# An unread F32 matmul behind each pair's channel transforms, with 71 to 64 columns

## The chip, the cores and the metric

The kernel runs on one core of a Trainium2 chip. The metric is the device time of one execution in microseconds (us). Profiled executions come with a trace of every instruction on the engines TensorE (PE; its weight loads are listed apart as PEld), VectorE (DVE), ScalarE (ACT), GpSimd (POOL) and SyncE (SP).

## The reference

```python
x = A_x                                    # (1, 2048, 512), float32
xn = _layernorm(x)
s = irfft2(rfft2(xn) * (A_w_r + 1j * A_w_i))      # over tokens and channels
h = _layernorm(xn)                         # inside the token MLP
u = gelu(einsum("bsd,sf->bdf", h, w1) + b1)       # w1: 2048 x 1792
y = einsum("bdf,fs->bds", u, w2) + b2             # w2: 1792 x 2048
out = x + s * silu(y.transpose(0, 2, 1))
```

Two things are computed from the same normalised tokens: a spectral filter (a two-dimensional FFT, a product with weights, and the inverse), and an MLP over the tokens, whose result gates the first.

## The kernel before

The 2048 tokens are 16 blocks of 128, the 512 channels stay whole. A first stage (to about 203 us) normalises the tokens, multiplies them with w1 into the hidden units, and does the token transforms and the filter of the spectral part between these products. From there on stands the last stage, with the second product of the MLP, the way back from channel frequencies to channels, the gates and the output.

The last stage (line 1038) is a loop over 8 pairs: pair p is the token blocks p and p + 8. For one pair the product with w2 is done in seven smaller products (names 1, 2, 5, 6, 3, 7, 4 of `ORDER`, line 800), sums of blocks of w2 against sums of blocks of the hidden units. `products` (line 905) issues one of them as 21 matmuls of 128 x 128 by 128 x 256: seven blocks of hidden units, each three times, since both sides are split into a high and a low part in F32R. In the trace these are `fa`, `fb`, `fc` or `fd` (hidden units) with `w2f` (the split weight). ScalarE and VectorE make the next `w2f` while TensorE works. The first two products of pair 0 are issued ahead of the loop.

Once in each pair, behind the product with the number `slot` (the 7th in pair 0, the 6th in pairs 1 to 6, the 4th in pair 7; `SLOTS`, line 38), TensorE does a few products in plain F32, in the order that `PARTS` (line 44) gives for the pair:

- E, `even_channels` (line 966): sixteen matmuls of 64 x 64 by 64 columns, `cd,yt` in the trace (`ci` is the tile `cd`, filled anew with other constants). Those of pair 0 are issued one product earlier (line 1075).
- S, `spectral` (line 1006): four matmuls of 64 x 64 by 512 columns for the pair before, `y,cft`. Pair 0 has none; pair 7's own come later (line 1096), ahead of its last product.
- O, `odd_channels` (line 977): four matmuls of 128 x 128 by 128 columns, `cd,yt`. They are the last of the group in every pair.

Then `unfolded` (line 984) reads the banks 6 and 7 of PSUM on ScalarE and VectorE, and from pair 1 on `finish` (line 1022) multiplies the pair before with its gates and adds it to the output by DMA. The seven products write the left halves (256 of 512 columns) of bank 4, of bank 5, and of bank 2 or 3 in turn (`banks`, line 902). The right half of bank 4 is not used in this stage.

In this stage instructions stand on each engine in the order in which they are written (`Kept`, line 131). Every instruction that goes through that helper has line 139 in the trace.

Of the kernel before, what the change touches and what calls it, by code (L numbers as in the profile page):

```python
# [141 lines left out]
def spectral_mixer_kernel(tc, x, w1, b1, w2, b2, wk, we, wx, c_f, c_ft, c_d, c_i, c_g, c_h, out):  # L142
    nc = tc.nc
    V, A, G, T, SY = nc.vector, nc.scalar, nc.gpsimd, nc.tensor, nc.sync
# [17 lines left out]
    with tc.tile_pool(name="ps", bufs=1, space=PSUM) as psp, ExitStack() as left, ExitStack() as right:  # L162
        ps = psp.tile([P, 8, 512], F32, name="ps")
# [297 lines left out]
        T = Kept(T, keep)  # L461
# [46 lines left out]
        for j in range(NJ):  # L508
# [25 lines left out]
            start, more_stats = j < 3, j + 3 < NJ  # L534
# [264 lines left out]
        NP, HD = NJ // 2, D // 2  # L799
# [38 lines left out]
        def sums_of_blocks():  # L838
            added_up("a12", "s1")
            added_up("a11", "a12")  # L840
# [36 lines left out]
        ci = cd  # L877
# [24 lines left out]
        def banks(p):  # L902
            return ps[:, 3 - p % 2, :HD], ps[:, 4, :HD], ps[:, 5, :HD]

        def products(p, n):

            wf = ready.pop(0)
            bx, by, bz = banks(p)
            o = {1: bx, 6: bx, 7: bx, 4: bx, 2: by, 5: bz, 3: bz}[n]

            for a, (wi, ui) in enumerate(((0, 0), (0, 1), (1, 0))):
                for m, i in enumerate(FORMS):
                    T.matmul(o, wf[:, wi, i], form_parts(n, i)[ui], start=m + a == 0 and n in (1, 2, 5),
                             stop=m == NH - 1 and a == 2, skip_group_check=n in (6, 3, 7, 4))

        def copied(name, src, where):
            t = where.tile([P, HD], F32, name=name, tag=name.split("_")[0], bufs=1)
            step(A.activation(t, src, AF.Copy))
            return t
# [21 lines left out]
        def new_sums(p):  # L941
            return (fp.tile([P, 2, 2, 2, P], F32, name=f"es{p}", tag="es"),
                    fp.tile([P, 2, 2, 2, P], F32, name=f"y{p}", tag="y"))

        def new_gates(p):
            return [fp.tile([P, D], F32, name=f"g{j}", tag="g", bufs=4) for j in (p, p + NP)]
# [6 lines left out]
        def gathered(p):  # L953


            yt = fp.tile([P, 2, 4, 2, 64], F32, name=f"yt{p}", tag="yt")
            yts[p] = yt
            for i, j in enumerate((p, p + NP)):
                for h in range(2):
                    to = yt[:, i, :, h ^ i].rearrange("p b (s c) -> p b s c", c=2)  # L960
                    yield V.tensor_copy(to, ey[:, :, h::2, j]) if i else A.activation(to, ey[:, :, h::2, j], AF.Copy)
# [4 lines left out]
        def even_channels(p):  # L966


            for i in range(2):
                for s in range(2):  # L970
                    at = slice(128 * i + 64 * s, 128 * i + 64 * s + 64)
                    for e in range(2):
                        for r, rows in enumerate((slice(0, 64), slice(64, P))):
                            T.matmul(ps[64 * e:64 * e + 64, 6 + r, at], yts[p][rows, i, 2 * s, e], ci[rows, 2 * s, :64],
                                     start=True, stop=True)
# [8 lines left out]
        def unfolded(p):  # L984

            es, y = new_sums(p) if p else first_sums
            e0, e1 = (es[:, :, k].rearrange("p i b c -> p i (b c)") for k in range(2))
            first, odd = ps[:, 6, :256].rearrange("p (i s c) -> p i s c", s=2, c=64), ps[:, 6:8, 256:]
            other = y.rearrange("p i h q c -> p (i h q c)")[:, :257]
            A.activation(other, ps[:, 7, :257], AF.Copy)  # L990
            other = other[:, :256].rearrange("p (i s c) -> p i s c", s=2, c=64)

            V.tensor_add(es[:, :, 1, :, :64], first, other)
            V.tensor_sub(es[:, :, 1, 0, :63:-1], first[:, :, 0], other[:, :, 0])
            V.tensor_sub(es[:, :, 1, 1, :63:-1], other[:, :, 1], first[:, :, 1])
            V.tensor_add(e0, e1, odd)
            V.tensor_sub(e1, e1, odd)
            yield
            u, v = es[:, :, :, 0], es[:, :, :, 1]
            V.tensor_add(y[:, :, :, 0], u, v)  # L1000
            yield
            V.tensor_sub(y[:, :, ::-1, 1], u, v)
            ys[p] = y.rearrange("p i h q c -> p i (h q c)")
            yield

        def spectral(p):

            y = ys.pop(p)
            for e, cols in enumerate((slice(0, 64), slice(64, P))):
                for r, rows in enumerate((slice(0, 64), slice(64, P))):  # L1010
                    i = e ^ r
                    T.matmul(ps[cols, i], cft[rows, cols], y[rows, i], start=True, stop=True)

        def gate(g, j, cols, src, scale):
            A.activation(g[:, cols], src, AF.Silu, bias=b2t[:, j:j + 1], scale=scale)

        def summed(name, a, b):
            t = fp.tile([P, HD], F32, name=name, tag="c", bufs=2)
            V.tensor_add(t, a, b)
            return t  # L1020
# [17 lines left out]
        for p in range(NP):  # L1038
            j0, j1 = p, p + NP
            more = p + 1 < NP  # L1040
            if p:
                gates[p] = new_gates(p)
            g0, g1 = gates[p]
            bx, by, bz = banks(p)
            slot, plan = SLOTS[min(p, 2) + (not more)]
            gathering = gathered(p)
            for k, n in enumerate(ORDER):
                started = not p and k < 2
                if not started:
                    products(p, n)  # L1050
                if n == 1 and p:
                    p1 = copied(f"p1_{p}", bx, w2p)
                elif n == 5:
                    p5 = copied(f"p5_{p}", bz, fp)
                elif n == 6:
                    v2 = copied(f"v2_{p}", bx, fp)
                elif n == 7:
                    c22 = summed(f"c22_{p}", bx, p5)
                if n == 3 and more:
                    c12 = summed(f"c12_{p}", bz, v2)  # L1060
                if not started:
                    ready.extend(w for w in [next(wforms, None)] if w is not None)
                if n == 2:
                    c11 = summed(f"c11_{p}", by, p1)
                elif n == 6:
                    gate(g0, j0, left_, c11, 1.0)
                elif n == 3 and more:
                    gate(g0, j0, right_, c12, 1.0)
                elif n == 7:
                    gate(g1, j1, right_, c22, -1.0)  # L1070
                elif n == 4:
                    for cols in (left_,) if more else quarter_rows:
                        gate(g1, j1, cols, bx[:, cols], -1.0)
                if not p and k == slot - 1:
                    even_channels(p)
                if k == slot:
                    for part in PARTS[p]:
                        {"S": spectral, "E": even_channels, "O": odd_channels}[part](p - (part == "S"))
                    yts.pop(p)
                    pieces = unfolded(p)  # L1080
                    if p:
                        for g, j in zip(gates.pop(p - 1), (j0 - 1, j1 - 1)):
                            finish(g, j, whole)
                for what in plan.get(k, ""):
                    next(gathering if what == "g" else pieces)
                if n == 3 and not more:
                    gate(g0, j0, right_, summed(f"c12_{p}", bz, v2), 1.0)
                if more and n == 7:
                    sums_of_blocks()
                if not more and k == 2:  # L1090
                    xr = [where.tile([P, NH * P], F32, name=f"xr{i}", tag="s1", bufs=1)[:, :D] for i, where in enumerate((w2p, fp))]
                    for to, j in zip(xr, (j0, j1)):
                        for rows, tokens in halved:
                            SY.dma_start(to[rows], x[tokens, j])
                if not more and k == 5:
                    spectral(p)
                    last_rows = fp.tile([P, 2, D], F32, name="rows", tag="yt")
                    finish(g0, j0, whole)
                    finish(g1, j1, right_)
# [38 lines left out]
```

## Time and profile before

| | |
|---|---|
| three runs, us | 365.52, 365.53, 365.69 |
| median | 365.53 |
| profiled execution, us | 365.77 |
| its span, first to last instruction | 364.0 |
| TensorE matmuls, busy | 358.1 us (98%), 3476 records |
| TensorE weight loads, busy | 310.8 us (85%) |
| VectorE, ScalarE, GpSimd, busy | 307.8, 211.2, 87.2 us |
| mean granted TensorE clock | 1.000 |

The profiled execution's own time is 1.77 us above its span. Busy times of matmuls overlap, and so do those of weight loads with matmuls: how fast TensorE moves is read from the starts of its instructions. One F32 matmul of the code can be several records of the trace; the count in a row of the order of instructions is that of the code, the count in a row of the trace that of the records.

### The profile page before, as it was taken

What the parts mean: (1) busy time and instruction counts of PE and PEld (TensorE: products, weight loads), DVE (VectorE), ACT (ScalarE), POOL (GpSimd) and SP (SyncE); (2) the same over time, 40 slices, a digit from 0 to 9 for tenths busy, and PEclk for the clock granted to TensorE, in tenths of its full rate; (3) what the DMA queues carried; (4) which work ended last, traced back from release to release, by engine and by line L of the source; (5) the groups of instructions that cost most, each with busy time, mean ns of one, the idle gap of its engine ahead of it and who ended that gap; (6) DMA issues with size and microseconds to landing.
All of it is one profiled execution on the core that took longest, in us unless ns stands there. A gap on an engine that the chain in (4) does not pass through costs nothing.

```text
span 364.0 us, 8851 instructions
## 1 busy us (share of the span) xinstructions
PE 358.1 (98%) x3476; PEld 310.8 (85%) x3476; DVE 307.8 (85%) x590; ACT 211.2 (58%) x385; POOL 87.2 (24%) x134
## 2 busy tenths in 40 slices
PE   8999999999999999999999999999999999999994
PEld 7788888888877778777888999989898989898993
DVE  5899999967699997999995988687887878797974
ACT  4877778867634426755237884655464546565431
POOL 4233333323222012220120001040503132130330
PEclk9999999999999999999999999999999999999999
DMA  7977999306695687996577288698888989898624
GB/s 207 246 190 187 231 288 333 133 0 155 172 275 181 189 241 193 252 239 201 174 236 156 101 236 172 180 185 200 189 184 212 178 224 164 240 162 209 114 27 90
DMA packets 33293, 68.66 MB, mean 189 GB/s; under 512 B 4612, under 2 KB 19380, under 8 KB 33124
## 3 DMA queue, kind: packets, MB, share of 16 engines
q1 hardware_dynamic: 24276, 42.44, 42.2%
q0 software_dynamic: 8496, 25.01, 32.0%
q10 hardware_dynamic: 480, 0.66, 0.6%
q8 instruction: 27, 0.44, 0.6%
q14 instruction: 14, 0.11, 0.1%
HBM read 59.70 MB, written 8.13 MB: 186 GB/s over the span
## 4 chain that ended last, share of the span: by engine, by line
PE 96%; DVE 1%; DMA 1%; issue 0%; ACT 0%; DVEq 0%
PE ps L139 96%; DMA x<-in_x_dram 1%; DVE stm L244 0%; DVE rows L139 0%; DVE h L469 0%; DVE w1l L469 0%; DVE h L272 0%; ACT g L139 0%; DVE v2m L221 0%; DVE mvm L220 0%; DVE tm L229 0%; ACT sdm L223 0%; DVEq L1134 0%; DVE r0m L228 0%; DVE nbm L237 0%
## 5 line engine op out<-in xcount | busy, mean ns | idle before, releaser
L139 PE MATMUL ps<-h,w1h 128*128 128x512 f32 x400 | 116.3, 397 | 0.1
L139 PEld LDWEIGHTS ps<-h,w1h 128*128 128x128 f32 x400 | 72.9, 188 | 19.9 <-issue 4.9
L139 PE MATMUL ps<-h,w1l 128*128 128x512 f32 x200 | 67.6, 390 | 0.0
L139 DVE TENSOR_TENSOR w2f<-a,w2f 128x896 fp32r<-128x896 f32 x36 | 39.2, 1090 | 16.4 <-ACT w2f L139 16.4
L139 ACT ACTIVATE w2f<-a 128x896 fp32r<-128x896 f32 x36 | 37.2, 1033 | 20.0 <-PE ps L139 7.6
L139 PEld LDWEIGHTS ps<-h,w1l 128*128 128x128 f32 x200 | 37.5, 188 | 8.1
L139 PE MATMUL ps<-fb,w2f 128*128 128x256 f32 x336 | 42.1, 280 | 0.0
L139 POOL DMA_DIRECT2D s<-in_w_dram x14 | 18.3, 1311 | 96.8 <-DMA s<-in_w_dram 71.7
L139 PE MATMUL ps<-fa,w2f 128*128 128x256 f32 x336 | 41.4, 278 | 0.0
L139 PEld LDWEIGHTS ps<-fb,w2f 128*128 128x128 f32 x336 | 39.9, 188 | 0.9 <-DVE c L139 0.8
L139 PE MATMUL ps<-fc,w2f 128*128 128x256 f32 x336 | 39.9, 277 | 0.0
L139 PEld LDWEIGHTS ps<-fa,w2f 128*128 128x128 f32 x336 | 39.9, 188 | 0.0
L139 PEld LDWEIGHTS ps<-fc,w2f 128*128 128x128 f32 x336 | 39.2, 188 | 0.0
L155 ACT ACTIVATE w1h<-w1s 128x512 fp32r<-128x512 f32 x26 | 16.2, 632 | 25.6 <-PE ps L139 10.8
L139 POOL DMA_DIRECT2D out_dram<-r x28 | 23.6, 1276 | 27.9 <-DVE r L139 27.9
L667 POOL DMA_DIRECT2D xc<-xc x16 | 9.8, 619 | 69.2 <-ACT xc L665 54.0
L308 POOL TENSOR_TENSOR ey<-t 128x256 f32<-128x256 f32 x16 | 15.7, 979 | 44.0 <-DVE t L306 44.0
L139 ACT ACTIVATE w2f<-s 128x896 fp32r<-128x896 f32 x15 | 15.3, 1022 | 14.2 <-PE ps L139 12.4
L139 DVE TENSOR_TENSOR w2f<-s,w2f 128x896 fp32r<-128x896 f32 x15 | 16.3, 1088 | 6.5 <-ACT w2f L139 6.4
L469 DVE TENSOR_TENSOR w1l<-w1r,w1h 128x384 fp32r<-128x384 f32 x32 | 21.3, 669 | 0.0
L139 PE MATMUL ps<-fd,w2f 128*128 128x256 f32 x168 | 20.7, 278 | 0.0
L268 ACT ACTIVATE h<-x,nbm,rsm 128x256 f32<-128x256 f32 (+1 forms) x34 | 18.4, 593 | 3.9 <-DVE nbm L263 3.1
(132 smaller groups left out, 602.3 us busy)
## 6 DMA issues: line engine op xcount, KB each, us to landing
a<-in_w_dram SPq DMA_DIRECT2D x22, 448.0 KB, 4.0
wt<-in_wk_dram POOLq DMA_DIRECT2D x16, 512.0 KB, 5.8
s<-in_w_dram SPq DMA_DIRECT2D x16, 448.0 KB, 4.1
s<-in_w_dram POOLq DMA_DIRECT2D x16, 448.0 KB, 6.5
w1s<-in_w_dram SPq DMA_DIRECT2D x52, 128.0 KB, 5.5
w1r<-in_w_dram SPq DMA_DIRECT2D x28, 192.0 KB, 5.1
xc<-xc POOLq DMA_DIRECT2D x16, 256.0 KB, 3.1
out_dram<-in_x_dram SPq DMA_DIRECT2D x4, 960.0 KB, 6.5
```

What stands on the lines that cost most here:

```text
L139: return lambda *args, **kw: self.keep(operation(*args, **kw))
L155: return A.activation(hi, src, AF.Copy), V.tensor_sub(lo, src, hi.bitcast(F32))
L268: keep(A.activation(to, v, AF.Identity, bias=m["nb"][:, i], scale=m["rs"][:, i, 1:2]))
L308: G.tensor_add(ey[:, 0::3, :, j], a, b)
L469: keep(V.tensor_sub(dst, src, hi.bitcast(F32)))
L667: keep(G.dma_start(*(v.rearrange("p s t c -> p s (t c)") for v in (there[c::2], here[1 - c::2, ::-1]))))
```

## The change

Two lines go into the loop over the pairs, right behind the channel transforms: one more F32 matmul of 128 x 128, with 71 columns in pair 0, 70 in pair 1, and so on to 64 in pair 7. Its operands are two of the four blocks of the constants `ci`, its target is the right half of bank 4, and nothing reads the result.

```diff
@@ -1077,6 +1077,8 @@
                     for part in PARTS[p]:
                         {"S": spectral, "E": even_channels, "O": odd_channels}[part](p - (part == "S"))
                     yts.pop(p)
+                    spare = ps[:, 4, HD:HD + 71 - p]
+                    T.matmul(spare, ci[:, 0], ci[:, 1, :spare.shape[1]], start=True, stop=True)
                     pieces = unfolded(p)
                     if p:
                         for g, j in zip(gates.pop(p - 1), (j0 - 1, j1 - 1)):
```

On TensorE, at the end of pair 0, the difference of the two orders reads so (`fb` with `w2f_0` is pair 0's last product, `fd` with `w2f_1` pair 1's first):

```order
 L139 MATMUL ps<-fb_2726,w2f_0_2828 128x256
 L139 MATMUL ps<-cd,yt_2834 128x128 x4
+L139 MATMUL ps<-cd 128x71
 L139 MATMUL ps<-fd_1426,w2f_1_2862 128x256 x2
 L139 MATMUL ps<-fd_1633,w2f_1_2862 128x256 x2
```

One instruction is added between the odd channels and the next product; nothing changes its place. In pair 2 TensorE has before, from the last matmul of the 6th product (`w2f_2_3284`) to the first ones of the 7th (`w2f_2_3315`):

```order
L139 MATMUL ps<-fb_2726,w2f_2_3284 128x256
L139 MATMUL ps<-cd,yt_3258 64x64 x16
L139 MATMUL ps<-y_3161,cft 64x512 x4
L139 MATMUL ps<-cd,yt_3258 128x128 x4
L139 MATMUL ps<-fb_1499,w2f_2_3315 128x256
```

The F32 group is even channels, spectral part and odd channels, and the F32R products follow. With the change (the numbers at the end of names are counted anew):

```order
L139 MATMUL ps<-fb_2726,w2f_2_3286 128x256
L139 MATMUL ps<-cd,yt_3260 64x64 x16
L139 MATMUL ps<-y_3163,cft 64x512 x4
L139 MATMUL ps<-cd,yt_3260 128x128 x4
L139 MATMUL ps<-cd 128x69
L139 MATMUL ps<-fb_1499,w2f_2_3317 128x256
```

The new matmul is the last of the F32 group, and the group is otherwise the same. So it is in pairs 1 to 7; on VectorE, ScalarE, GpSimd and SyncE the instructions stand as before.

## The prediction

> **What bounds the kernel now.** I read the totals by engine first, then the chain of work that ended last, then TensorE's waits, and last the timeline of TensorE in the pairs, which are what the change touches.
>
> ```profile
> PE 358.1 (98%) x3476; PEld 310.8 (85%) x3476; DVE 307.8 (85%) x590; ACT 211.2 (58%) x385; POOL 87.2 (24%) x134
> ```
>
> ```profile
> 9.34 350.07 PE ps L139 x3439
> 359.42 0.02 issue
> 359.44 0.38 ACT g L139
> 359.82 0.02 issue
> 359.84 0.75 DVE rows L139 x3
> ```
>
> ```profile
> PE ps L139 <- POOL wz L443: 1.1, 1, 1.1
> ```
>
> The first fence is the page's busy time, the second the end of the chain in order of time, the third the only wait that the trace gives TensorE. A busy share proves little by itself, since matmuls overlap, but the chain does: from 9.34 to 359.41 us it is nothing but TensorE's own queue, 96% of the span, and its single wait lies at the start. Whatever is put into this queue is paid in full, and so is any change in how fast the queue moves. What follows it (one gate on ScalarE, three steps on VectorE, the last DMAs) shifts along unchanged.
>
> How fast it moves is not the same everywhere. Here are the same instructions of the timeline in pair 1 and in pair 2 (start, time, engine, shapes, count; a row ends with the drain of its last matmul, so I use starts alone).
>
> ```profile
> 238.20 1.16 PE L139 MATMUL ps<-cd,yt 128*128 128x128 f32 x8
> 239.12 2.72 PE L139 MATMUL ps<-fb,w2f 128*128 128x256 f32 x21
> 241.68 2.63 PE L139 MATMUL ps<-fd,w2f 128*128 128x256 f32 x21
> 244.15 2.63 PE L139 MATMUL ps<-fa,w2f 128*128 128x256 f32 x21
> ...
> 254.04 2.63 PE L139 MATMUL ps<-fb,w2f 128*128 128x256 f32 x21
> 256.61 0.69 PE L139 MATMUL ps<-cd,yt 64*64 64x64 f32 x32
> 257.12 1.04 PE L139 MATMUL ps<-y,cft 64*64 64x512 f32 x8
> 258.09 1.16 PE L139 MATMUL ps<-cd,yt 128*128 128x128 f32 x8
> 259.01 2.63 PE L139 MATMUL ps<-fb,w2f 128*128 128x256 f32 x21
> 261.47 2.54 PE L139 MATMUL ps<-fd,w2f 128*128 128x256 f32 x21
> ...
> 273.37 2.54 PE L139 MATMUL ps<-fb,w2f 128*128 128x256 f32 x21
> 275.85 0.69 PE L139 MATMUL ps<-cd,yt 64*64 64x64 f32 x32
> ```
>
> From 241.68 to 254.04 us lie 105 matmuls of 256 columns (five products of 21), 0.1177 us each. From 261.47 to 273.37 us lie the same 105, 0.1133 us each. The step changed by 4.4 ns (0.46 us over 105), and it changed at one place: behind the F32 channel transforms of pair 2, where the queue comes back to the F32R products. No engine was waited for there. The table by stretches says which pairs have which step (matmuls running in 10 us, in brackets; clock 1.00 throughout).
>
> ```profile
> 224.00:234.00 10.00, 10.00 (x87) 1.00 0.66 161
> 242.00:252.00 10.00, 10.00 (x87) 1.00 0.91 176
> 262.00:272.00 10.00, 10.00 (x90) 1.00 0.91 182
> 281.00:291.00 10.00, 10.00 (x90) 1.00 0.91 167
> 300.00:310.00 10.00, 10.00 (x91) 1.00 0.89 166
> 320.00:330.00 10.00, 10.00 (x91) 1.00 0.89 179
> 337.00:347.00 10.00, 10.00 (x91) 1.00 0.60 98
> ```
>
> ```profile
> 350.44 2.72 PE L139 MATMUL ps<-fa,w2f 128*128 128x256 f32 x21
> 353.00 2.63 PE L139 MATMUL ps<-fb,w2f 128*128 128x256 f32 x21
> 355.64 1.09 PE L139 MATMUL ps<-y,cft 64*64 64x512 f32 x8
> ```
>
> So the step is long behind the transforms of pairs 0 and 1, short behind those of pairs 2 to 6, and long again behind those of pair 7 (a product of 21 takes 2.63 there, as in pair 1). It is fixed at the exit from a stretch of F32 products and kept until the next such stretch. The clock and the DMA load don't decide it. The new product stands exactly at these eight exits.
>
> **The change part by part.** *The products themselves.* A call of F32 runs as two passes: the 32 calls of the odd channels (four in each of eight pairs) are 64 records.
>
> ```profile
> L139 PE MATMUL ps<-cd,yt 128*128 128x128 f32 x64 | 9.2, 286 | 0.0
> ```
>
> That makes 8 x 2 = 16 passes. The Trainium skill (FP8 and Floating Point Precision, TensorE Precision Notes) gives true FP32 four passes; the trace has two records for a call, and with 32 passes at the price below the term would be 3.55 us instead of 1.78.
>
> What a pass costs is its weight load, not its columns. Two answers on weight loads show it, from the odd channels of pair 2 and from the warm-up:
>
> ```profile
> 258.09 0.97 PEld L139 LDWEIGHTS ps<-cd,yt 128*128 128x128 f32 x8 [0.81 <-issue]
> 258.98 0.42 PEld L139 LDWEIGHTS ps<-fb,w2f 128*128 128x128 f32 x3
> ```
>
> ```profile
> 5.86 0.41 PEld L139 LDWEIGHTS ps<-wz 128*128 128x128 f32 x3
> ```
>
> ```profile
> 5.97 0.30 PEld L139 LDWEIGHTS ps<-wz 128*128 128x128 f32 x2
> ```
>
> Eight loads of 128 columns start in 0.89 us, 0.111 each. The warm-up's loads also start 0.11 apart, though their F32R matmul of 128 columns should stream in about half the 0.1133 us of the 256-column one. So a matmul shorter than its load gains nothing, and 71 columns or 64 cost the same: 16 x 0.111 = 1.78 us, all on the chain. The bounds: were a pass as short as a round of four small F32 matmuls of 64 columns (eight rounds from 256.61 to 257.12 us, 0.064 each), 16 x 0.064 = 1.02 us; were the first load of each product not hidden, 8 x 0.111 more, 2.67 us. I take 1.78, since the load of 128 columns is the same instruction in the same place. Below nothing it can't be, as no wait on TensorE could swallow it. [...]
>
> *No new wait.* Both operands are the constants that the odd channels already use, the 71 columns lie in the unused half of bank 4, and nothing reads them. VectorE's and ScalarE's work on the transforms starts when it did, because it hangs on the odd channels' last pass. Its work for the next product (the split weight) has 0.22 us more time.
>
> *The step behind the exits.* This is the larger term. Pairs 2 to 6 look like a loop that repeats itself exactly: the F32R products behind the transforms start at 259.01 us in pair 2 and in the pairs after it at
>
> ```profile
> 278.25 2.63 PE L139 MATMUL ps<-fb,w2f 128*128 128x256 f32 x21
> 297.49 2.63 PE L139 MATMUL ps<-fb,w2f 128*128 128x256 f32 x21
> 316.73 2.63 PE L139 MATMUL ps<-fb,w2f 128*128 128x256 f32 x21
> 335.97 2.63 PE L139 MATMUL ps<-fb,w2f 128*128 128x256 f32 x21
> ```
>
> 19.24 us apart each time. Having come out with the short step once, they come out with it again because everything between two exits lasts the same. The other exits, reached with other lengths, all have the long step: of four distinct approaches (pair 0, pair 1, the loop, pair 7) one is short. Two extra passes, 0.22 us, shift every approach. As an estimate from the steps themselves: 0.1133 and 0.1177 us fit as 17 and 17 2/3 parts of 6.67 ns, a pass as 16.7 of them; two passes are then 33.4 parts, about half a part off a whole number, as far from where the loop closes as it can be. So I expect the short step to be lost in pairs 2 to 6 and not found in the others.
>
> Behind the exits of pairs 2 to 5 stand 7 x 21 = 147 matmuls up to the next F32 stretch, behind that of pair 6 five products, 105: together 588 + 105 = 693, and 693 x 4.4 ns (0.46 / 105) = 3.04 us.
>
> *The sum.* The profiled execution took 365.77 us: a span of 364.0 and 1.77 around it. 365.77 + 1.78 + 3.04 = 370.59. It lay 0.24 above the median of the three runs (365.53), so I forecast 370.4.
>
> **The rivals.** *The steps stay as they are.* The exits may depend on something that two passes don't shift; for it speaks that each new pass has the length of the eight before it. Then 365.77 + 1.78 = 367.55, less 0.24: 367.3.
>
> *A mixture.* If the column count enters the length of a pass at all, the pairs with 71 to 64 columns shift by different amounts, and some exits come out short, some long. Against it speak the load rows. Each of the five short stretches that is lost costs 147 x 4.4 ns = 0.64 us (pair 6: 0.46); with two or three lost it is 368.6 to 369.2. A pass paid by its columns, 0.064 us, belongs here too: with steps unchanged 365.77 + 1.02 - 0.24 = 366.6. [...]
>
> *All exits become short: not slower.* The place is the exits of pairs 0, 1 and 7, which now have 126 + 147 + 42 = 315 long steps behind them. If the shifted approach is one from which every exit comes out short, they give back 315 x 4.4 ns = 1.38 us, and 365.77 + 1.78 - 1.38 - 0.24 = 365.9, within 0.2% of before. It decides only if all eight go that way; from five short stretches on without the others the run is slower. One in four of the approaches seen was short, and the half part speaks against it.
>
> *Work that vanishes.* Were an unread product left out, nothing would change; it stands in the order of TensorE's instructions at all eight places, so I give this nothing.
>
> **How the numbers follow.** All exits long 0.42 (370.4); a mixture 0.28 (367.3 to 370.4); steps as before 0.16 (367.3); all short 0.08 (365.9); passes paid by columns with old steps 0.04 (366.6). A measurement of this kernel can tell about 0.2% (0.73 us) from no change. All short lies within it; faster than that would need cheap passes and all exits short at once, 365.2, and even that lies within, so 0.02 is left for a cause that I don't see. The range runs from 367.1 (steps as before, 0.2 to spare) to 370.9 (all long, with part of the dearer load), and leaves out the last two cases.
>
> **What would show it.** In the profile after: 16 more TensorE records; weight loads 0.11 us apart through the odd channels and the new product; and, above all, products of 21 that start 2.47 us apart (87 matmuls in 10 us) in pairs 2 to 6, where they were 2.38 (90 or 91). If pairs 2 to 6 keep 2.38, the idea that the exit's approach decides is wrong or the passes don't shift it; if pairs 0 or 1 turn to 2.38, the rival of short exits gains. If the loads of the new product start closer than 0.1 us, its price was wrong.

## The result, and the profile after

The changed kernel takes 370.52 us (median of three runs, 370.46 to 371.47) where the kernel before took 365.53. The ratio of the means is 1.0143, 95% interval 1.0118 to 1.0168. Its profiled execution took 370.52 us too, with a span of 368.7 us, 4.7 above the span before.

The end of its chain in order of time, and TensorE's only wait:

```profile
9.27 354.89 PE ps L139 x3455
364.16 0.02 issue
364.18 0.38 ACT g L139
364.56 0.02 issue
364.58 0.75 DVE rows L139 x3
```

```profile
PE ps L139 <- POOL wz L443: 1.1, 1, 1.1
```

TensorE still waits for nobody, and what follows it is as long as before. The 4.8 us that the chain gained (354.89 against 350.07) are all in its own queue. The timeline of pair 2 after, to be laid beside that of pair 2 before:

```profile
258.52 1.16 PE L139 MATMUL ps<-cd,yt 128*128 128x128 f32 x8
259.51 0.34 PE L139 MATMUL ps<-cd 128*128 128x69 f32 x2
259.66 2.72 PE L139 MATMUL ps<-fb,w2f 128*128 128x256 f32 x21
262.21 2.63 PE L139 MATMUL ps<-fd,w2f 128*128 128x256 f32 x21
...
274.58 2.63 PE L139 MATMUL ps<-fb,w2f 128*128 128x256 f32 x21
```

The new product is two records. And the 105 matmuls from 262.21 to 274.58 us take 12.37 us, 0.1178 each: the long step, where pair 2 had 0.1133 before. The table by stretches has it in pairs 2 to 6 (88 matmuls in 10 us, and 78 in the 9 us of the last row, where these pairs had 90 or 91 in 10 us). Pairs 0 and 1 (87 in 10 us) and pair 7 (36 in 4 us) have the long step as before.

```profile
262.00:272.00 10.00, 10.00 (x88) 1.00 0.92 175
282.00:292.00 10.00, 10.00 (x88) 1.00 0.91 159
302.00:312.00 10.00, 10.00 (x88) 1.00 0.92 157
322.00:332.00 10.00, 10.00 (x88) 1.00 0.94 163
342.00:351.00 9.00, 9.00 (x78) 1.00 0.54 88
```

The weight loads of the same place give the product's own price:

```profile
258.52 0.97 PEld L139 LDWEIGHTS ps<-cd,yt 128*128 128x128 f32 x8 [0.81 <-issue]
259.40 0.30 PEld L139 LDWEIGHTS ps<-cd 128*128 128x128 f32 x2
259.63 2.54 PEld L139 LDWEIGHTS ps<-fb,w2f 128*128 128x128 f32 x21
```

Two loads from 259.40 to 259.63 us: 0.11 each, as for the eight before them. From one pair to the next the two terms can be added up again:

```profile
259.66 2.72 PE L139 MATMUL ps<-fb,w2f 128*128 128x256 f32 x21
279.77 2.72 PE L139 MATMUL ps<-fb,w2f 128*128 128x256 f32 x21
299.88 2.72 PE L139 MATMUL ps<-fb,w2f 128*128 128x256 f32 x21
319.99 2.72 PE L139 MATMUL ps<-fb,w2f 128*128 128x256 f32 x21
340.10 2.72 PE L139 MATMUL ps<-fb,w2f 128*128 128x256 f32 x21
```

The pairs are 20.11 us apart instead of 19.24. The 0.87 more are 0.22 for the product and 0.65 for 147 steps.

### The profile page after: what moved, and what is told of

Read it like the earlier page. It is cut to its first block, busy times and chain, and to the rows that moved or that the text cites. A ratio compares the mean times of both kernels' runs of the same rounds, so it can differ in the third digit from the quotient of the medians.

```text
span 368.7 us, 8883 instructions
## 1 busy us (share of the span) xinstructions
PE 363.0 (98%) x3492; PEld 316.0 (86%) x3492; DVE 308.3 (84%) x590; ACT 211.4 (57%) x385; POOL 87.1 (24%) x134
## 4 chain that ended last, share of the span: by engine, by line
PE 98%; DVE 0%; ACT 0%; POOL 0%; issue 0%; DVEq 0%; POOLq 0%
PE ps L139 98%; DVE rows L139 0%; ACT g L139 0%; POOL wz L443 0%; DVEq L1136 0%; POOLq L1129 0%
## 5 line engine op out<-in xcount | busy, mean ns | idle before, releaser
L139 PE MATMUL ps<-fb,w2f 128*128 128x256 f32 x336 | 42.9, 282 | 0.0
L139 PE MATMUL ps<-fa,w2f 128*128 128x256 f32 x336 | 42.2, 280 | 0.0
L139 PEld LDWEIGHTS ps<-fb,w2f 128*128 128x128 f32 x336 | 40.7, 188 | 0.9 <-DVE c L139 0.8
L139 PE MATMUL ps<-fc,w2f 128*128 128x256 f32 x336 | 40.9, 279 | 0.0
L139 PEld LDWEIGHTS ps<-fa,w2f 128*128 128x128 f32 x336 | 40.7, 188 | 0.0
L139 PEld LDWEIGHTS ps<-fc,w2f 128*128 128x128 f32 x336 | 40.1, 188 | 0.0
```

The lines of the kernel that those rows point to most:

```text
L139: return lambda *args, **kw: self.keep(operation(*args, **kw))
```

## The experiments

Theory A (alignment): the step behind an exit depends on where in a fine grid (parts of about 6.67 ns, the prediction's estimate) the F32 group ends, and one new product moves that by half a part. Theory B: any extra product behind the transforms loses the short step. Theory C: the new product is paid by its columns. The kernel before took 365.65 to 365.72 us (medians) beside these runs, and each ratio is to its mean. Where starts are given to the nanosecond, they are those that the kept traces hold; the rows shown are rounded to 0.01 us.

### How many products

```diff
-                    spare = ps[:, 4, HD:HD + 71 - p]
+                    spare = ps[:, 4, HD:HD + 128]
```

> One product at every exit, 128 columns in each pair instead of 71 to 64. Theory A, with the weight load as the price: nothing changes against 71 to 64 columns, 370.5 us, all pairs with the long step, and 0.22 us for each product. Theory C (columns pay): 16 passes get some 60 columns longer; if a pass of 64 columns is 0.064 us and one of 128 is 0.111, the earlier price was about 1.1 and this one is 1.78, so about 371.2 us against 370.5.

Measured: 370.52 us, 1.0130 (1.0115 to 1.0145), the same as with 71 to 64 columns. Columns below the width of the load were free here, and theory C falls. That agrees with the load rows. The Trainium skill (TensorE: Matmul & The Clock Gate, Back-to-back issue gap) gives a gap by columns, N / 2.4 + 2.5 ns, for a matmul by itself; as an estimate, 60 columns more in 16 passes would by it cost 0.4 us. For a stream of loads and matmuls the same section has both of them set the spacing, so the formula is not the one for this place, and the equal times bear that out.

```diff
+                    for _ in range(2):
-                    T.matmul(spare, ci[:, 0], ci[:, 1, :spare.shape[1]], start=True, stop=True)
+                        T.matmul(spare, ci[:, 0], ci[:, 1, :spare.shape[1]], start=True, stop=True)
```

> Two of the new products behind each other at every exit instead of one (same columns, 71 to 64). Theory A (alignment): one product moves the exit by about half a part of a grid of 6.67 ns, so two move it by a whole number and pairs 2 to 6 come out with the short step again: 365.5 + 32 x 0.111 = 369.1 us, that is faster than with one product, and 90 or 91 matmuls in 10 us in pairs 2 to 6. Theory B (any extra product behind the transforms loses the short step): 365.5 + 3.55 + 3.04 = 372.1 us, 87 or 88 matmuls in 10 us everywhere.

Measured: 369.24 us, 1.0094 (1.0077 to 1.0111). Twice the added work is 1.28 us faster than the work once. The table by stretches (pairs 0 to 5) shows why: pairs 0 and 1 long, and the short step back from pair 2 on.

```profile
224.00:234.00 10.00, 10.00 (x87) 1.00 0.69 152
243.00:253.00 10.00, 10.00 (x87) 1.00 0.88 176
263.00:273.00 10.00, 10.00 (x90) 1.00 0.89 179
283.00:293.00 10.00, 10.00 (x91) 1.00 0.91 182
303.00:313.00 10.00, 10.00 (x91) 1.00 0.86 175
```

Theory B falls. Since the steps are those of the kernel before, the run also gives the price alone: 369.24 - 365.65 = 3.59 us for 32 passes, 0.112 each.

The same with `range(3)`:

> Three of the new products behind each other at every exit (71 to 64 columns as in the kernel after). Theory A: an odd number of products is half a part off, an even one is not, so with three the pairs 2 to 6 lose the short step again as with one: 365.65 + 48 x 0.112 + 3.08 = 374.1 us, 87 or 88 matmuls in 10 us everywhere. If the kernel with two was a chance hit: the short step stays, 365.65 + 5.37 = 371.0 us.

Measured: 374.13 us, 1.0233 (1.0219 to 1.0247), and the long step in every pair:

```profile
262.00:272.00 10.00, 10.00 (x87) 1.00 0.84 148
304.00:314.00 10.00, 10.00 (x87) 1.00 0.87 154
328.00:338.00 10.00, 10.00 (x87) 1.00 0.79 191
```

One product loses the short step, two keep it, three lose it. So the hit with two was hardly chance. The size of the move is read from the starts in the traces: with two products the F32R products behind the exits of pairs 2 to 6 start 19.687 us apart, against 19.240 in the kernel before. The 0.447 us are 67.0 parts of 6.67 ns for two products, 33.5 for one if both cost the same. That fits half a part.

```diff
-                    spare = ps[:, 4, HD:HD + 71 - p]
-                    T.matmul(spare, ci[:, 0], ci[:, 1, :spare.shape[1]], start=True, stop=True)
+                    spare = ps[:, 4, HD:HD + 130]
+                    T.matmul(spare, ci[:, 0], ci.rearrange("p b c -> p (b c)")[:, 128:258], start=True, stop=True)
```

> One product at every exit, 130 columns in each pair. With two columns more than the load the matmul itself should set the pass, an F32 column taking 0.111 / 128 = 0.87 ns at most: a pass is 1.7 ns longer than with 128 columns, two passes 3.3 ns, which is half of the grid's 6.67 ns. Theory A: together with the half part of the two passes that makes a whole number, pairs 2 to 6 keep the short step, and the time is 365.5 + 1.8 = 367.3 us, 3 us below the kernel with 128 columns. Theory B: 370.5 us as with 128.

Measured: 370.50 us, 1.0126 (1.0111 to 1.0141), long steps everywhere. Theory A's forecast missed. That two columns lengthen the F32 group by half a part was my assumption, and it doesn't hold. In pair 2 it is 2.832 us from the last F32R matmul ahead of the group to the first one behind it, with 130 columns as with 128 (2.609 before the change). The two columns moved the exit no further than 128 columns do, so the long steps don't speak against the theory, and the run tests it no further.

### One pair alone

```diff
+                    if p == 2:
-                    spare = ps[:, 4, HD:HD + 71 - p]
-                    T.matmul(spare, ci[:, 0], ci[:, 1, :spare.shape[1]], start=True, stop=True)
+                        spare = ps[:, 4, HD:HD + 71 - p]
+                        T.matmul(spare, ci[:, 0], ci[:, 1, :spare.shape[1]], start=True, stop=True)
```

> The new product in pair 2 alone (69 columns), none in the other seven pairs. Theory A: pair 2 comes out with the long step; pair 3 is then reached as pair 1 or pair 2 were before, so the short step is found again one or two pairs later: 365.5 + 0.22 + 0.64 = 366.4 us, or 367.0 with two pairs lost. Theory B1 (the short step is a state that, once lost, stays lost): 365.5 + 0.22 + 3.04 = 368.8 us. Theory B2 (only the pair with the product is touched, and nothing is carried along): 366.4 us with pairs 3 to 6 short.

Measured: 366.53 us, 1.0019 (1.0010 to 1.0029), 0.88 above the kernel before. Pair 2 is long, and from pair 3 on the step is short:

```profile
242.00:252.00 10.00, 10.00 (x87) 1.00 0.91 182
262.00:272.00 10.00, 10.00 (x87) 1.00 0.89 174
282.00:292.00 10.00, 10.00 (x91) 1.00 0.91 177
302.00:312.00 10.00, 10.00 (x90) 1.00 0.89 182
```

So one lost exit doesn't lose the rest (B1 falls): a product costs the short step of its own pair, and the 3 us are five such pairs. A and B2 give the same here; the counts above tell them apart.

### The same work in another order

In the kernel before, without any new product:

```diff
-PARTS = ("O", *["ESO"] * 6, "SEO")
+PARTS = ("O", "SEO", *["ESO"] * 5, "SEO")
```

> The kernel before, without any new product; only the order of pair 1's channel transforms is changed, spectral part, even channels, odd channels, as in pair 7, instead of even, spectral, odd. The same work. Theory A: pair 1's exit is reached with another alignment. In the kernel with the new products pair 7, in this order and after long steps, had its odd channels where pairs 2 to 6 have them when the short step follows; so pair 1 should come out with the short step and hand it on to pair 2 and the loop: 147 x 4.4 ns = 0.64 us less than before, 364.9 us. Theory B (the step is lost or found by what stands behind the transforms, order within them is nothing): 365.5 us.

Measured: 365.15 us, 0.9985 (0.9976 to 0.9993): a little faster than the kernel before, with the same instructions, and faster than the changed one. Pair 1 has the short step (second row), and hands it on:

```profile
224.00:234.00 10.00, 10.00 (x87) 1.00 0.72 162
242.00:252.00 10.00, 10.00 (x91) 1.00 0.91 178
262.00:272.00 10.00, 10.00 (x91) 1.00 0.87 183
282.00:292.00 10.00, 10.00 (x90) 1.00 0.86 186
```

```diff
-PARTS = ("O", *["ESO"] * 6, "SEO")
+PARTS = ("EO", *["ESO"] * 6, "SEO")
...
-                if not p and k == slot - 1:
-                    even_channels(p)
```

> The kernel before; pair 0's even channels are issued in one group with its odd channels instead of one product earlier. The same work. One entry into F32 and one exit less: the exit at 218.31 us costs 0.226 - 0.118 = 0.11 us more than a step, so some 0.1 us less. Theory A: pair 0's exit is reached with another alignment, which no trace shows; if it is the short step's, pairs 0 and 1 gain 273 x 4.4 ns = 1.2 us (364.2 us); if not, pair 1's approach changes too and the time is 365.4 us, or 366.1 if pair 2 loses the short step for one pair. Theory B: 365.4 us.

Measured: 366.69 us, 1.0063 (1.0036 to 1.0091). The steps behind the F32 groups are as before, but I had overlooked a wait: pair 0's last product needs a bank that VectorE still reads, and the even channels had covered that. Now TensorE stands still for 0.61 us ahead of it.

```profile
218.47 2.62 PE L139 MATMUL ps<-fb,w2f 128*128 128x256 f32 x21 [0.61 <-DVE c L139]
```

Four of its nine executions took about 3.1 us more than the other five (369.6 to 369.8 against 366.4 to 366.7), as much as the short step is worth in pairs 2 to 6. Those four have no trace, so that they lost it is argued and not shown. The trace has something else that I had not looked for: behind this wait the matmuls of the product start 113 or 114 ns apart, where those ahead of it start 117 to 119 ns apart. So the step can change at a wait too, with no F32 product in between.

Both changes of order together:

> Both changes of order together. Theory A: if pair 0's exit comes out long as before, pair 1 has the short step or not by where pair 0's stretch ends: 364.8 us or 365.4 us; if pair 0's exit comes out short, pair 1 in the order of pair 7 is reached like pair 7 before, which came out long: 364.8 us (pair 0 short, pair 1 long). Theory B: 365.4 us.

Measured: 365.86 us, 1.0003 (0.9995 to 1.0012). The time missed by the wait just named; the step is short from pair 1 on, and the kernel is 0.6 us below the undisturbed executions with pair 0's change alone.

### One matmul more ahead of the transforms

In the kernel before, at the end of pair 1's sixth product:

```diff
+                    for _ in range(1 if p == 1 else 0):
+                        u = form_parts(n, FORMS[0])[0]
+                        T.matmul(ps[:, 4, HD:], u[:, :P], u, start=True, stop=True)
                     for part in PARTS[p]:
```

> The kernel before with one more matmul in all: an unread F32R one of 128 x 128 by 256 columns, at the end of pair 1's sixth product, just ahead of the channel transforms. Theory A: with long steps the starts go through three alignments in turn (three steps are 353.3 ns, 53 parts of 6.67 ns). One step more makes pair 1's stretch end on the alignment on which pair 2's ends in the kernel before, and pair 2 comes out short; so pair 1 comes out short too and hands it on: 0.12 us for the matmul, 147 x 4.4 ns = 0.64 us back, 365.65 - 0.52 = 365.1 us. More work, less time. Theory B (the step has nothing to do with where the stretch ends): 365.8 us, and pair 2 first to be short.

Measured: 365.86 us, 1.0004 (0.9996 to 1.0013): the price of the matmul and no more, with pair 2 first to be short. Theory A's forecast missed. This matmul took weights and columns from one tile, which none of the matmuls of `products` does. So I made it one of their kind, inside `products`:

```diff
+            if p == 1 and n == 7:
+                T.matmul(ps[:, 4, HD:], wf[:, 1, FORMS[0]], form_parts(n, FORMS[0])[0], start=True, stop=True)
```

> The kernel before with one unread F32R matmul of 256 columns at the end of pair 1's sixth product, this time with that product's own split weight as its weights, so that it is one more of the same kind; in the earlier attempt weights and columns came from the same tile, and pair 1 stayed long. Theory A: pair 1's stretch ends on the alignment of pair 2's, pair 1 comes out short: 365.7 + 0.12 - 0.64 = 365.2 us. If where the stretch ends decides nothing, 365.85 us as in the earlier attempt.

Measured: a median of 365.18 us, in nine of eleven executions 365.0 to 365.4; two took 369.4 and 370.3, so the interval of the ratio lies on both sides of 1 (1.0009, 0.9978 to 1.0041). The trace shows pair 1 short:

```profile
224.00:234.00 10.00, 10.00 (x88) 1.00 0.71 163
242.00:252.00 10.00, 10.00 (x91) 1.00 0.92 175
262.00:272.00 10.00, 10.00 (x90) 1.00 0.91 180
```

One useless matmul more, and nine times in eleven half a microsecond less. What the first attempt had that this one lacks is the shared tile; that it is this which moved the alignment wasn't tried apart.

Two such matmuls (of the first kind) ahead of pair 0's odd channels:

> The kernel before with two more matmuls of that kind, at the end of pair 0's last product, ahead of its odd channels. Theory A gives no sure forecast: two steps more put pair 0's exit on an alignment that no trace has shown so far, between those that came out short and long. If it is short: 0.24 us for the matmuls, 273 x 4.4 ns = 1.2 us back in pairs 0 and 1, 364.7 us. If it is long: pair 1's stretch may end elsewhere too, 365.9 us, or 365.3 us if pair 1 then comes out short. Theory B: 365.9 us.

Measured: a median of 365.37 us, 1.0001 (0.9984 to 1.0017; one execution of twelve took 369.0). Pair 0 came out long, pair 1 short, the third of the cases in the expectation.

### A smaller load

```diff
-                    spare = ps[:, 4, HD:HD + 71 - p]
-                    T.matmul(spare, ci[:, 0], ci[:, 1, :spare.shape[1]], start=True, stop=True)
+                    spare = ps[:64, 4, HD:HD + 64]
+                    T.matmul(spare, ci[:, 0, :64], ci[:, 1, :64], start=True, stop=True)
```

> The kernel after, with the new product's weights cut to 64 columns (64 x 64 outputs instead of 128 x 71 to 64). If the weight load is the price, a pass falls from 0.111 to about 0.058 us (a round of small F32 matmuls, with loads of 64 columns, takes 0.064): the product costs 0.12 instead of 0.22 us, 8 x 0.10 = 0.8 us less than with the kernel after. Theory A: two such passes, 0.117 us, are 17.5 parts of 6.67 ns, again half a part off, so pairs 2 to 6 stay long: 370.5 - 0.8 = 369.7 us. If the matmul's columns are the price: 370.5 us. Theory B: 369.7 us.

Measured: 368.73 us, 1.0085 (1.0072 to 1.0098). The total lies below every forecast, but the price rose. Weight loads in pair 2:

```profile
258.43 0.97 PEld L139 LDWEIGHTS ps<-cd,yt 128*128 128x128 f32 x8 [0.81 <-issue]
259.52 0.19 PEld L139 LDWEIGHTS ps<-cd 128*64 128x64 f32 x2
259.78 2.00 PEld L139 LDWEIGHTS ps<-fb,w2f 128*128 128x128 f32 x17
```

From the first load of the odd channels to the first of the next product it is 1.35 us, against 0.89 before the change and 1.11 after: the product costs 0.46 us and not 0.12. The small load starts 1.09 us after the first of the eight instead of 0.88. Theory A's forecast of long steps was worked out from the lower price and falls with it. This other length leaves the short step in place, and finds it in pair 1 too:

```profile
242.00:252.00 10.00, 10.00 (x91) 1.00 0.92 163
262.00:272.00 10.00, 10.00 (x90) 1.00 0.91 176
```

8 x 0.46 - 0.64 = 3.0 us above 365.68, as measured. So my price by the size of the load was wrong as a rule, and right only for a load like its neighbours. Why the smaller one costs more, no run here shows.

The run also speaks against a rival to theory A, that each added product simply turns the step over, whatever its length (one loses it, two keep it, three lose it). Here one product of two records is added, as in the changed kernel, and the short step stays. By the starts in the trace, pairs 2 to 6 are 19.693 us apart: the product adds 0.453 us, 68.0 parts, a whole number as with two products of the full load.

## Why the prediction was right

- *The queue of TensorE is the bound, and no wait takes up what is added.* So it is: the chain and the waits after are those of before, 4.8 us longer.
- *Sixteen passes at 0.111 us, 1.78 us, whatever their columns.* The load rows after show 0.11, the kernel with two products 0.112, and 128 columns cost the same as 71 to 64. That a load sets the price holds for a full load between full loads; the run with 64 columns of weights shows that it can't be scaled down. The Trainium skill (FP8 and Floating Point Precision, TensorE Precision Notes) gives a true F32 product four passes. The trace has two records for one, and 0.11 us is the price of a record; whether a record holds more than one such pass, no run here shows.
- *The exits lose the short step: 693 x 4.4 ns = 3.04 us.* The pairs 2 to 6 have the long step after, 0.65 us for 147 matmuls. Taking the price measured with two products from the whole, 370.52 - 365.53 - 1.79 = 3.20 us is left for this term; within the two profiled executions, whose chains differ by 4.82 us, it is 3.03.
- *Half a part off.* This was the weakest step, an estimate from three durations. It was also partly luck: the load rows, read to 0.01 us (0.88 to 0.90 for eight loads), allow 33.0 to 33.8 parts for two passes, and only the starts to the nanosecond gave 33.5. One, two and three products came out as it says. 130 columns didn't, since they moved nothing; why the first extra matmul in pair 1 didn't is open. That the alignment decides is the account that fits the most runs here, with no run that sets it directly. What sits on the 6.67 ns grid, no run here shows.
- *The sum.* 370.59 us from the profiled execution, against 370.52 in the one after. Taking 0.24 us off for the median was of no use: after the change the profiled execution lies on the median.

The rivals fell one by one: the steps as they are by the table after, the mixture and all exits short by the same table, and the price by columns by the run with 128. But an exit of pair 1 that comes out short does exist, at no cost, with its transforms in another order.

## What to carry to other kernels

When one engine's queue is the whole chain, compare the distance between starts of like instructions over the whole run before pricing an edit: two steps for the same work are a term that a small insertion can switch on or off, here 3 us beside 1.8 us of added work. Whether an insertion, a reorder or a doubling helps then has to be measured, and a repeat that loses the gain in some executions is a reason to prefer the variant that never did: the reorder of pair 1 stayed between 364.8 and 365.5 us in all its eleven executions. And a smaller matmul need not be cheaper: here the one with a load like its neighbours' was, and the smaller one cost twice as much.

## What the runs showed of the hardware that I had not expected

- F32R matmuls of 128 x 128 by 256 columns, with no engine waited for and the granted clock at 1.00, run at one of two steps, 0.1133 or 0.1178 us. In the last stage the step changed only at a group of F32 matmuls or, in the two kernels with pair 0's channels in one group, at a wait of TensorE (0.61 us); in between it stayed.
- Which of the two it is can be changed by work that nobody reads: eight products more cost 5.0 us, sixteen 3.6 us.
- A product with weights of 64 columns between full ones cost 0.46 us, where one with 128 cost 0.22.
